# Other planning constants and thresholds in a four-layer attention kernel whose instruction order a planner lays out

## The chip, the cores and the metric

The kernel runs on one core of a Trainium2 chip. The core has five engines that run side by side and meet only at semaphores: TensorE (PE; matrix products, with PEld its weight loads), VectorE (DVE), ScalarE (ACT), GpSimd (POOL) and SyncE (SP). The metric is the device time of one execution in microseconds. Before the change it is 1484.73 us, the median of three runs (1484.37 to 1490.2).

## The reference

Four layers run over one sequence of 2048 rows of 512 columns, each with a layer norm in front and added to its input: softmax attention with 32 query heads of width 16 that share one key head and one value head (A), linear attention (B), and the same two once more.

```python
def _A_ref(x, wq, wk, wv, wo):
    q = heads(x @ wq)                  # 32 heads of 16
    k, v = x @ wk, x @ wv              # one head of 16 each
    scores = einsum("bhqd,bkd->bhqk", q, k) * 16 ** -0.5
    p = softmax(scores)
    return merge(einsum("bhqk,bkd->bhqd", p, v)) @ wo

def _B_ref(x, wqkv, wo):               # phi(t) = t + 1 if t > 0 else exp(t), plus 1e-6
    q, k, v = split_heads(x @ wqkv)
    kv, z = einsum("bhsd,bhse->bhde", phi(k), v), phi(k).sum(rows)
    return merge(phi(q) @ kv / (phi(q) @ z + 1e-6)) @ wo

x = x + _A_ref(layernorm(x), A_wq, A_wk, A_wv, A_wo)
x = x + _B_ref(layernorm(x), B_wqkv, B_wo)
x = x + _A_ref(layernorm(x), A_wq, A_wk, A_wv, A_wo)
x = x + _B_ref(layernorm(x), B_wqkv, B_wo)
```

Layers 0 and 2 (A) hold most of the work: each has 32 x 2048 x 2048 exponentials.

## The kernel before

**Blocks and segments.** An A layer is cut into blocks of 128 keys by 512 (head, query) columns, 2048 blocks a layer, 4096 in all. A segment (`Seg`, L356) holds the blocks of one query tile of 128 rows and one half of the heads, 64 blocks as a rule; in layer 2 the first tiles are cut into smaller ones. For each block TensorE makes the scores with an array cut by rows (L990, "row" mode, 32x128 tiles, up to four products at a time), an engine takes the exponential, and TensorE multiplies by V with an array cut by columns (L1044, "col" mode, 128x32 tiles, four products at a time) into one accumulator bank. Other products use the whole array ("full").

**Two ways to an exponential.** ScalarE takes groups of two or three blocks from a set of three PSUM banks in one instruction (L1170, output in PT buffers). VectorE takes single blocks: it adds a constant to the scaled score and writes the result as a 16-bit integer whose bits are a power of two in bf16 (L1256, output in FB buffers). That is coarse, so four shifted copies with weights 0.35, 0.30, 0.25 and 0.21 are summed: four VectorE blocks make a chunk of 128x2048, and three copies of the chunk are made with 32, 64 and 96 added to the integers. TensorE multiplies all four copies by weighted V tiles (VW). A VectorE block thus costs four value products and a ScalarE block one.

**Who makes the copies.** VectorE makes them with one instruction each (L1304). One of the three may be made by a transfer instead: GpSimd first issues a transfer that fills a buffer with the constant (`prime`, L1316, issued at L1328), and once the chunk is whole, a transfer that adds the chunk to it on the way (`dma_shift`, L1335, issued at L1337). This document calls the second one an addition. Each is 512 KB.

**The planner.** No engine decides anything on the chip. While the program is built, `Planner` (L36) plays the run through with a set duration for each operation, keeps a queue by priority for each engine, and writes down for each engine the order in which its operations started. That order is what the chip runs, with semaphores between the engines. So the constants in question never reach the chip; they change which engine takes a block, and the order. Constants the change touches:

- `SWITCH` (L384, used at L179): what TensorE is charged when the array's shape changes. A QK group is charged 0.22, a value group 0.222.
- `DXF` (L450) and `DTAIL` (L451), used at L1329 and L1338: how long an addition holds the transfer queue, and what passes after that until it has landed. Issue is charged 0.95 and a latency of 0.3, a prime holds the queue for 1.7. The reload of a weight (L676) uses `DTAIL` too.
- `TUNE` (L454), thresholds for layer 0 and layer 2. They are module globals; what layer 0 sets and layer 2 doesn't stays in force in layer 2 (L1098, L1100).

The thresholds, by what they decide:

- Whether VectorE takes a block. In place of the third block of a ScalarE group (`dve_split`, L1246): only if VectorE's urgent backlog is at most `BLS` and its whole backlog at most `BLT`. With a bank of its own beside a group (`dve_open`, L1240): backlog at most `BLO`. Alone (`alone`, L1266, called at L144): backlog at most `DXB`. A new chunk is opened only with more than `FBO` free buffers (L1229).
- From where it takes the block (`dve_pick`, L1207): from the end of a segment that is more than `CHT` blocks ahead of ScalarE (`ENDL` in the last segment), or, if the four column groups are uneven, more than `CHE`.
- When the copies are made (L1295): a copy waits while at most `FBS` buffers are free and segments ahead of it still have value products to issue (for small segments, more than `AHEAD` of them).
- Whether a copy becomes an addition (L1291): a buffer must be primed, the chunk must not lie in the last `DMIN` segments, and the planned transfer queue must be less than `DQ` us long. A buffer is primed (L1323) only if fewer than `NPRE` are, more than `FBP` are free, and ScalarE isn't in the last `DMIN` segments.
- `BACK` (L1116): how many segments before the end two borrowed weight buffers are called back. `STICK` (L166): by how much priority TensorE may be pulled from, to stay in the present one of "col" and "full". `LAG` (L70) keeps its value.

```python
if len(blk) == CHB and primed and si < len(segs) - DMIN and pl.dmaq < pl.now + DQ:
    ws.remove(DSH)
    dma_shift(blk, f_, hold, *primed.pop(0))
```

There are 18 buffers of a chunk's size at most (12 of them FB, the others borrowed from OBB, sacc, xn, wq and wo2 while those rest; traces name them so).

When TensorE would idle, the planner puts in products whose result nobody uses (`fill`, L1070, issued at L1089), so that the array doesn't fall silent.

Of the kernel before, what the change touches and what calls it, by code (L numbers as in the profile page):

```python
# [35 lines left out]
class Planner:  # L36
# [43 lines left out]
    def op(self, opts, reads=(), writes=(), prio=5.0, lat=0.08, dma=False, name="", join=None, mode="full", port=False, after=(), behind=(), xfer=None, trn=False):  # L80

        o = Op()
        o.opts, o.prio, o.users, o.done, o.end = opts, prio, [], False, None
        o.eng, o.fn, o.n, o.value, o.sem, o.signal, o.isdma = None, None, None, None, None, False, dma
        o.name = (name, lat)
        o.freed = False
        o.begun = None
        o.cols = 0
        o.mode = mode
        o.port = port  # L90
        o.xfer = xfer
        o.trn = trn
        deps = set()
        for k in reads:
            deps.update(self.ws(k))
        for k in list(writes) + list(after) + list(behind):
            deps.update(self.ws(k))
            deps.update(self.readers.get(k, ()))
        if join is not None:
            deps.update(join.deps)  # L100
            deps.discard(join)
        for k in writes:
            if join is not None and join in self.ws(k):
                self.writer[k] = self.ws(k) + [o]
            else:
                self.writer[k] = [o]
                self.readers[k] = []
        for k in list(reads) + list(after):
            if k not in writes:
                self.readers.setdefault(k, []).append(o)  # L110
        o.deps = deps
        o.left = 0
        chain = len(opts) == 1 and PE in opts
        for d in deps:
            if not (d.done or (chain and d.freed and d.eng == PE)):
                o.left += 1
                d.users.append(o)
        if o.left == 0:
            self._eligible(o)
        return o  # L120
# [26 lines left out]
    def _dispatch1(self, e):  # L147
# [4 lines left out]
        while h:  # L152
# [24 lines left out]
            if e == PE:  # L177
                if self.mode != o.mode:
                    dur += max(SWITCH - (self.now - self.until[e]), ROWIN if o.mode == "row" else 0.0)  # L179
                self.mode = o.mode  # L180
# [175 lines left out]
class Seg:  # L356
# [11 lines left out]
    def take(self, js, back=False):  # L368
# [12 lines left out]
QK_DUR = 0.22  # L381
PV_DUR = 0.222
QK_LAT = 0.438
SWITCH = 0.107  # L384
ROWIN = 0.025
PV_LAT = 0.215
EX_LAT = 0.185
# [3 lines left out]
LAG = 0.15  # L391
# [17 lines left out]
BLS = 1.4  # L409
BLO = 5.0  # L410
DXB = 2.0
BLT = 2.5
# [12 lines left out]
ENDL = 12  # L425
# [7 lines left out]
FBO = 2  # L433
FBS = 4
AHEAD = 20
CHT = 19
PSH = False
STICK = 0.8
PBL = 1.2
BACK = 2  # L440
PRING = 8
DSH = 1
DMIN = 4
NPRE = 2
EVEN = True
CHE = 8
AVOID = True
PGEN = 0.95
DPF = 1.7
DXF = 3.2  # L450
DTAIL = 2.0  # L451
DQ = 4.0
FBP = 4
TUNE = {0: {"CHE": 2, "AHEAD": 10, "BLS": 1.7, "FBP": 2, "NPRE": 1, "DMIN": 3, "LAG": 0.1, "STICK": 2.0, "FBO": 1, "FBS": 4, "BLO": 7.0, "DXB": 0.8, "BLT": 3.2},  # L454
        2: {"CHE": 6, "CHT": 16, "FBS": 2, "AHEAD": 15, "BLO": 3.5, "DXB": 2.5, "FBP": 3, "DMIN": 2, "STICK": 0.8, "LAG": 0.1, "DQ": 5.0}}


def bass_interleave_layers__grouped_kv_mqa__linear_attn_block__prompt_kernel(
# [111 lines left out]
    def guest(L, kind, i, h=None):  # L570
        return once((L, kind, i, h), home[kind, i]) if (kind, i) in home else ()
# [103 lines left out]
    def reload(dst, src, writes, prio, behind):  # L675
        return op({PO: (1.1, lambda e: e.dma_start(dst, src))}, writes=writes, prio=prio, lat=0.3, dma=True, behind=behind, xfer=(2.4, DTAIL))  # L676

# [34 lines left out]
    def fb_keys(i):  # L712
        return [("FB", i, h) for h in range(CHB)]
# [267 lines left out]
    def run_a(L):  # L981
# [23 lines left out]
        def spend(h, o):  # L1005
            h[0] -= 1
            if o not in h[1]:
                h[1].append(o)
            if h[0] == 0:
                pl.give_after(h[2], h[3], h[1])  # L1010
# [85 lines left out]
        def act_stream():  # L1096
            if L == 0:
                globals().update(TUNE[0])  # L1098
            yield ("flag", ("K", L, 0))
            globals().update(TUNE[L])  # L1100
            if L:
# [214 lines left out]
        def prime():  # L1316
# [6 lines left out]
            while state["si"] < len(segs) - DMIN:  # L1323
                if len(primed) >= NPRE or len(fb_pool.free) <= FBP or fb_pool.wait:
# [3 lines left out]
                o = op({PO: (PGEN, lambda e, g_=g_: e.dma_start(fbs[g_].bitcast(I16), cst.to_broadcast([P, CHB * 512])))}, reads=["cst"], writes=fb_keys(g_), prio=9.0,  # L1328
                       lat=0.3, dma=True, behind=guest(L, "FB", g_), xfer=(DPF, DTAIL))  # L1329
                primed.append((g_, o))  # L1330
# [4 lines left out]
        def dma_shift(blk, f_, hold, g_, o):  # L1335
            pl.stat["dma"] += 1
            o = op({PO: (PGEN, lambda e: e.dma_start(fbs[g_].bitcast(I16), fbs[f_].bitcast(I16), accum_op=ALU.add))}, reads=fb_keys(f_), writes=fb_keys(g_), prio=0.0, lat=0.3,  # L1337
                   dma=True, xfer=(DXF, DTAIL))  # L1338
            spend(hold, o)
# [601 lines left out]
```

## Time and profile before

| | before |
|---|---|
| median of 3 runs (lowest, highest) | 1484.73 us (1484.37, 1490.2) |
| profiled execution: its time / its span | 1484.35 us / 1482.5 us |
| busy: PE, DVE, ACT, POOL | 95%, 95%, 97%, 29% of the span |
| mean granted TensorE clock | 1.000 |
| exponentials on ScalarE (L1170) | 1364 instructions of two or three blocks, 1374.3 us |
| blocks on VectorE (L1256) | 1131 |
| copies by VectorE (L1304) | 639 |
| additions (L1337) / primes (L1328) | 216 / 218 |

How to read it: a line such as "L1337 POOL DMA_DIRECT2D" is the group of instructions that line 1337 of the kernel made on GpSimd. "x110" counts instructions, then follow busy time in us and the mean of one in ns, then the idle time of the engine right before them and what ended it. Instructions overlap: on ScalarE and VectorE the next one starts before the last one has written its end, so the time from start to start is shorter than the time of one. The view of windows gives each engine's busy time between two moments; asked for one line, it gives that line's. The chain of waits lists the work that ended last, piece by piece: start, us that the piece set the pace, engine, tile, line, count.

### The profile page before, as it was taken

Reading aid. Unit: us, or ns where it says so; the run is one execution under the profiler, and the core shown is the slowest. Engines: PE = TensorE matmul, PEld = TensorE weight load, DVE = VectorE, ACT = ScalarE, POOL = GpSimd, SP = SyncE. Lnnn points to the kernel's source line nnn. Section 1 sums busy time; section 2 is a strip of 40 time slices with the busy share of each in tenths; the row PEclk is TensorE's granted clock in tenths of the full one; section 3 lists DMA queues with packets and bytes.
Section 4 is the critical chain, followed back from the end, with each engine's and each line's share of the span. In section 5 each row is a group of like instructions: output and inputs, shape, how many; then the busy total and the mean of one; then the engine's idle time right before and its main releaser. Section 6 shows DMA issues by size and latency. Waiting matters only on the chain.

```text
span 1482.5 us, 40513 instructions
## 1 busy us (share of the span) xinstructions
PE 1415.0 (95%) x16387; PEld 512.6 (35%) x16387; DVE 1412.3 (95%) x2628; ACT 1441.2 (97%) x1536; POOL 424.9 (29%) x627
## 2 busy tenths in 40 slices
PE   7999999999999999999999999999999999999998
PEld 4433333333332323233644323333333333333235
DVE  7999999999999999998866899999999999999996
ACT  8999999999999999999799999999999999999996
POOL 5323333333333332300111223333323333223201
PEclk9999999999999999999999999999999999999999
DMA  4887898897888987710000458898879899879701
GB/s 116 229 205 194 185 212 188 203 215 179 195 204 197 217 192 168 187 43 2 2 2 2 104 136 200 201 211 205 212 188 226 201 211 215 203 183 216 172 1 58
DMA packets 76745, 240.14 MB, mean 162 GB/s; under 512 B 14993, under 2 KB 20113, under 8 KB 76562
## 3 DMA queue, kind: packets, MB, share of 16 engines
q0 software_dynamic: 62928, 229.14, 65.9%
q1 hardware_dynamic: 13634, 8.43, 2.0%
q8 instruction: 131, 2.15, 0.6%
q14 instruction: 52, 0.43, 0.1%
HBM read 120.62 MB, written 2.10 MB: 83 GB/s over the span
## 4 chain that ended last, share of the span: by engine, by line
PE 38%; DVE 35%; ACT 19%; issue 7%; POOL 1%; DMA 0%; ACTq 0%; DVEq 0%; POOLq 0%
PE ps L1044 15%; DVE FB L1256 14%; ACT PT L1170 12%; PE ps L990 12%; DVE FB L1304 7%; ACT xnT L1170 3%; PE ps L761 3%; PE ps L923 2%; PE ps L1089 2%; ACT OBB L1170 2%; PE ps L1410 2%; DVE wq L1256 1%; DVE xn L1256 1%; DVE sacc L1390 1%; PE ps L757 1%
## 5 line engine op out<-in xcount | busy, mean ns | idle before, releaser
L1170 ACT ACTIVATE PT<-ps 128x1024 bf16<-128x1024 f32 (+1 forms) x957 | 1004.8, 1163 | 5.4 <-PE ps L990 4.5
L1256 DVE TENSOR_SCALAR FB<-ps 128x512 int16<-128x512 f32 x852 | 558.0, 677 | 2.4 <-PE ps L990 1.6
L990 PE MATMUL ps<-QT,KM 32*128 32x512 bf16 x4096 | 534.6, 384 | 26.7 <-ACT PT L1170 14.9
L1044 PE MATMUL ps<-FB,VW 128*32 128x512 bf16 x3279 | 471.5, 385 | 10.9 <-ACT PT L1170 4.2
L1044 PE MATMUL ps<-PT,V 128*32 128x512 bf16 x2081 | 375.2, 386 | 4.0 <-DVE FB L1304 1.3
L990 PEld LDWEIGHTS ps<-QT,KM 32*128 32x128 bf16 x4096 | 134.2, 90 | 445.7 <-ACT PT L1170 216.0
L1170 ACT ACTIVATE xnT<-ps 128x1024 bf16<-128x1024 f32 (+1 forms) x240 | 261.0, 1162 | 1.0 <-PE ps L990 0.5
L1304 DVE TENSOR_SCALAR FB<-FB 128x2048 int16<-128x2048 int16 (+1 forms) x346 | 230.7, 674 | 0.0
L1337 POOL DMA_DIRECT2D FB<-FB x110 | 105.0, 955 | 334.3 <-DVE FB L1256 176.5
L1170 ACT ACTIVATE OBB<-ps 128x1024 bf16<-128x1024 f32 (+1 forms) x167 | 186.3, 1151 | 0.7 <-PE ps L990 0.6
L1044 PEld LDWEIGHTS ps<-FB,VW 128*32 128x32 bf16 x3279 | 115.8, 94 | 147.7 <-issue 81.3
L1328 POOL DMA_DIRECT2D FB<-shift_row x150 | 124.6, 831 | 45.2 <-PE ps L1044 23.9
L1089 PE MATMUL ps<-QT,V 128*32 128x512 bf16 (+6 forms) x548 | 132.7, 311 | 1.7 <-DVE sacc L1393 0.9
L1044 PEld LDWEIGHTS ps<-PT,V 128*32 128x32 bf16 x2081 | 91.3, 93 | 65.4 <-issue 36.7
L1044 PE MATMUL ps<-xnT,V 128*32 128x512 bf16 x522 | 105.1, 386 | 0.3 <-ACT PT L1170 0.3
L844 POOL TENSOR_SCALAR ve<-mv 128x1 f32<-128x1 f32 x64 | 29.5, 463 | 234.2 <-DVE mv L843 232.6
L1044 PE MATMUL ps<-OBB,V 128*32 128x512 bf16 x362 | 82.5, 387 | 1.8 <-ACT PT L1170 0.8
L761 PE MATMUL ps<-wqkv,xnT 128*32 128x512 bf16 x960 | 83.2, 383 | 0.8 <-DVE xnT L746 0.7
L1089 PEld LDWEIGHTS ps<-QT,V 128*32 128x32 bf16 x548 | 44.1, 95 | 56.8 <-issue 35.1
L1256 DVE TENSOR_SCALAR xn<-ps 128x512 int16<-128x512 f32 x80 | 52.7, 677 | 0.0
L1044 PE MATMUL ps<-xn,VW 128*32 128x512 bf16 x267 | 49.7, 385 | 1.8 <-ACT PT L1170 1.3
L1256 DVE TENSOR_SCALAR wq<-ps 128x512 int16<-128x512 f32 x75 | 49.3, 676 | 0.1
(221 smaller groups left out, 1805.8 us busy)
## 6 DMA issues: line engine op xcount, KB each, us to landing
FB<-shift_row POOLq DMA_DIRECT2D x150, 512.0 KB, 6.7
FB<-FB POOLq DMA_DIRECT2D x110, 512.0 KB, 6.0
sacc<-shift_row POOLq DMA_DIRECT2D x17, 512.0 KB, 6.9
wq<-shift_row POOLq DMA_DIRECT2D x16, 512.0 KB, 7.1
wo<-shift_row POOLq DMA_DIRECT2D x14, 512.0 KB, 7.1
xn<-shift_row POOLq DMA_DIRECT2D x14, 512.0 KB, 7.1
FB<-wq POOLq DMA_DIRECT2D x13, 512.0 KB, 6.1
wq<-FB POOLq DMA_DIRECT2D x12, 512.0 KB, 6.1
```

The lines of the kernel that those rows point to most:

```text
L761: ins = e.matmul(dst[c, :], lhsT=l[:, c], rhs=r, start=(k == 0), stop=(k == len(pairs) - 1))
L844: op({PO: (0.1, lambda e: e.tensor_scalar(out=ve[:, t:t + 1], in0=mv[:, t, 1:2], scalar1=1e-5, scalar2=None, op0=ALU.add))}, reads=[("mv", ...
L923: ins = e.matmul(dst[:, g * P:(g + 1) * P], lhsT=lhs(g, k), rhs=rhs(k), start=(k == 0), stop=(k == FT - 1))
L990: return e.matmul(bank(b), lhsT=KM[r, sg.par, kt * P:(kt + 1) * P], rhs=QT[r, sg.t, :], start=True, stop=True)
L1044: ins = e.matmul(ps[32 * j:32 * j + 32, ACC * 512:(ACC + 1) * 512], lhsT=V[:, kt, :] if w is None else VW[:, kt, w, :], rhs=ap, start=(k = ...
L1089: o = op({PE: (n / 2400.0, lambda e: e.matmul(ps[32 * j:32 * j + 32, b * 512:b * 512 + n], lhsT=V0[:], rhs=QT[:, sg.t, 0:n], start=st, sto ...
L1170: ex = op({AC: (0.051 + 0.4267 * n, lambda e, n=n, s_=s_, p_=p_: e.activation(pts[p_][:, 0:n * 512], ps[:, s_ * 512:(s_ + n) * 512], ACTF. ...
L1256: o = op({DV: (0.602, lambda e: e.tensor_scalar(out=dst.bitcast(I16), in0=bank(b), scalar1=VB, scalar2=VLO, op0=ALU.add, op1=ALU.max))}, w ...
L1304: o = op({en: (du, lambda e, w=w, g_=g_: e.tensor_scalar(out=fbs[g_][:, 0:n].bitcast(I16), in0=fbs[f_][:, 0:n].bitcast(I16), scalar1=float ...
L1328: o = op({PO: (PGEN, lambda e, g_=g_: e.dma_start(fbs[g_].bitcast(I16), cst.to_broadcast([P, CHB * 512])))}, reads=["cst"], writes=fb_keys ...
L1337: o = op({PO: (PGEN, lambda e: e.dma_start(fbs[g_].bitcast(I16), fbs[f_].bitcast(I16), accum_op=ALU.add))}, reads=fb_keys(f_), writes=fb_k ...
L1410: o = op({PE: (0.12, lambda e, c=c: e.transpose(ps[:, b * 512 + c * P:b * 512 + (c + 1) * P], src[:, c * P:(c + 1) * P], identF[:]))}, rea ...
```

## The change

Constants alone change. In the planner `SWITCH` goes from 0.107 to 0.112, `DXF` from 3.2 to 3.0 and `DTAIL` from 2.0 to 1.8; `TUNE` gets other thresholds. The description of the change gives 194 additions for the new order.

```diff
-SWITCH = 0.107
+SWITCH = 0.112
...
-DXF = 3.2
-DTAIL = 2.0
+DXF = 3.0
+DTAIL = 1.8
...
-TUNE = {0: {"CHE": 2, "AHEAD": 10, "BLS": 1.7, "FBP": 2, "NPRE": 1, "DMIN": 3, "LAG": 0.1, "STICK": 2.0, "FBO": 1, "FBS": 4, "BLO": 7.0, "DXB": 0.8, "BLT": 3.2},
-        2: {"CHE": 6, "CHT": 16, "FBS": 2, "AHEAD": 15, "BLO": 3.5, "DXB": 2.5, "FBP": 3, "DMIN": 2, "STICK": 0.8, "LAG": 0.1, "DQ": 5.0}}
+TUNE = {0: {"CHE": 4, "FBO": 1, "FBS": 2, "AHEAD": 10, "BLS": 1.0, "DXB": 1.6, "BLT": 3.2, "NPRE": 1, "STICK": 1.5, "BACK": 3, "ENDL": 6, "FBP": 5, "DMIN": 3, "DQ": 4.0, "LAG": 0.1},
+        2: {"CHE": 4, "FBO": 0, "BLO": 3.5, "FBP": 6, "DMIN": 4, "ENDL": 12, "FBS": 7, "DXB": 1.2, "DQ": 3.0}}
```

With what stays in force from layer to layer and from the defaults, the values that differ are:

| | layer 0 before | layer 0 after | layer 2 before | layer 2 after |
|---|---|---|---|---|
| CHE / CHT / ENDL | 2 / 19 / 12 | 4 / 19 / 6 | 6 / 16 / 12 | 4 / 19 / 12 |
| BLS / BLO / DXB | 1.7 / 7.0 / 0.8 | 1.0 / 5.0 / 1.6 | 1.7 / 3.5 / 2.5 | 1.0 / 3.5 / 1.2 |
| FBO / FBS / FBP | 1 / 4 / 2 | 1 / 2 / 5 | 1 / 2 / 3 | 0 / 7 / 6 |
| DMIN / DQ | 3 / 4.0 | 3 / 4.0 | 2 / 5.0 | 4 / 3.0 |
| AHEAD / STICK / BACK | 10 / 2.0 / 2 | 10 / 1.5 / 3 | 15 / 0.8 / 2 | 10 / 1.5 / 3 |

## Prediction

> **What bounds the kernel now.** I read the page's busy times first, then the windows of the two long stages in which VectorE takes blocks, then the same windows for single lines, and last the chain of waits and the list of waits.
>
> ```profile
> PE 1415.0 (95%) x16387; PEld 512.6 (35%) x16387; DVE 1412.3 (95%) x2628; ACT 1441.2 (97%) x1536; POOL 424.9 (29%) x627
> ...
> PE 38%; DVE 35%; ACT 19%; issue 7%; POOL 1%; DMA 0%; ACTq 0%; DVEq 0%; POOLq 0%
> ```
> ```profile
> 100.00:650.00 550.00, 528.30 (x6098) 171.19 (x6095) 547.76 (x982) 548.27 (x570) 170.90 (x225) 1.00 0.81 190
> 850.00:1400.00 550.00, 531.42 (x6197) 177.38 (x6197) 548.32 (x998) 546.81 (x578) 179.07 (x236) 1.00 0.85 200
> ```
>
> The second fence is the view of windows: a stretch of 550 us in layer 0 and one in layer 2, with the busy time of PE, PEld, DVE, ACT and POOL, the granted clock, the share of the DMA engines and GB/s. DVE and ACT are busy for 99.4 to 99.7% of both, the clock is 1.00, and transfers stay off the chain (DMA 0%). TensorE only looks nearly as full: its dummy products (L1089) run where it has nothing else to do, 61.38 and 49.58 us in the two stretches:
>
> ```profile
> 100.00:650.00 550.00, 61.38 (x262) 21.09 (x262) 1.00 0.81 190
> 850.00:1400.00 550.00, 49.58 (x207) 16.64 (x207) 1.00 0.85 200
> ```
>
> So two engines share 2048 blocks a layer and neither has a hole. The length of these stages is the work of ScalarE and VectorE over what both can do, and an order can shorten them only by making that work smaller. The four next rows are of the stage of layer 0 and that of layer 2, for the additions (L1337) and VectorE's copies (L1304), then the totals for VectorE's blocks (L1256) and ScalarE's exponentials (L1170):
>
> ```profile
> 41.00:701.60 660.60, 104.29 (x109) 1.00 0.76 178
> 832.00:1445.00 613.00, 102.39 (x107) 1.00 0.79 185
> 41.00:701.60 660.60, 224.44 (x335) 1.00 0.76 178
> 832.00:1445.00 613.00, 199.20 (x304) 1.00 0.79 185
> 41.00:701.60 660.60, 387.13 (x592) 1.00 0.76 178
> 832.00:1445.00 613.00, 350.07 (x537) 1.00 0.79 185
> sum 1482.50, ACT 1374.28; mean ACT 274.86
> ```
>
> They close: in layer 0, 592 blocks are 148 chunks of four, with three copies each 444, and 335 + 109 = 444. VectorE takes 592 + 537 and two more between the stages, 1131, and ScalarE the other 4096 - 1131 = 2965.
>
> **The change part by part.** *Prices.* The chain of waits shows VectorE's operations start to start:
>
> ```profile
> 652.40 0.60 DVE sacc L1501
> 653.00 1.39 DVE FB L1304 x2
> 654.39 1.19 DVE FB L1256 x2
> 655.58 0.60 DVE FB L1304
> 656.18 1.20 DVE FB L1256 x2
> ```
>
> A block and a copy of a chunk cost 0.60 us each. A block on VectorE with all three copies made there costs (4 + 3) x 0.60 / 4 = 1.05 us; a block on ScalarE costs 1374.28 / 2965 = 0.46 us.
>
> *Fewer additions.* Of 109 + 107 = 216 additions 194 would be left, 22 fewer. `DMIN` in layer 2 accounts for some: two more segments of 613 / 32 = 19 us without additions, at 107 in 613 us, are 7. The rest would come from `FBP` (fewer primes) and `DQ` (3.0 for 5.0). Each one dropped is a copy for VectorE, 22 x 0.60 = 13.2 us. Nothing hides that, since VectorE has 2 us of idle in 550. It is shared, though: if VectorE gives y blocks to ScalarE, both end later by 0.46 y = 13.2 - 1.05 y, so y = 8.7 and the end moves by 4.0 us, a share of 0.31 of any work added to VectorE (0.69 for ScalarE). Bounds: 1.3 us if only `DMIN`'s 7 count (7 x 0.60 x 0.31), 4.0 for all 22; I take 4.0, since the count is given. GpSimd loses 44 issues, and TensorE 8.7 x 3 / 4 value groups, about 1.4 us; both have room.
>
> *Shorter planned transfers.* An addition is planned to land 0.95 + 0.3 + 3.2 + 2.0 = 6.45 us after it starts, behind an empty queue, and after the change 6.05. The view of line L1337 and the list of waits say:
>
> ```profile
> who waited for it (us, times):
>   PEld ps L1044: 0.2, 1
> ...
> DMA to landing us min/median/max: 4.6/6.0/9.1
> ```
> ```profile
> PEld ps L1044 <- DVE FB L1304: 17.3, 64, 0.8
> ```
>
> Today TensorE waits once, 0.2 us, for an addition. Planned 0.4 us earlier, value products move up by as much, and about half the landings (those above the median, 6.0) come after the plan. In TensorE's order the score products for the next group stand behind such a wait, and ScalarE waits for those. Lower bound nothing; upper bound 97 waits of 0.4 us, 39 us. TensorE waits 17.3 us for VectorE's copies today, the same kind of wait, while ScalarE is idle 4.9 us in the 1100 of the two stretches whatever the cause, so at most 39 x 4.9 / 17.3 = 11 us would reach ScalarE, 8 us of time. I take 1 us, near the row of 0.2. The Trainium skill, DMA: Bandwidth & Descriptors, section "Anatomy of one DMA — SWDGE (gpsimd) path", fits 2.0 us plus bytes / 436e3 us to such a transfer, which for 512 KB is an estimate of 3.2 us; by it both plans are pessimistic and this term is nothing, a sum 1 us lower. The trace disagrees, at a median of 6.0.
>
> *Shape changes.* In the chain near 50 us TensorE's pieces are
>
> ```profile
> 50.54 0.32 PE ps L990 x3
> 50.87 0.33 PE ps L1044 x4
> 53.85 0.76 PE ps L1044 x12
> 55.59 0.55 PE ps L1044 x8
> ```
>
> One, two and three groups of four cost 0.33, 0.55 and 0.76, so a group is 0.215 and the change of shape 0.11. The plan's score group with its switch goes from 0.220 + 0.107 = 0.327 to 0.332, against 0.32: 5 ns on each change, on an engine with 111 us of dummy products in the two stretches. Nothing.
>
> *Backlog thresholds* (`BLS`, `BLO`, `DXB`). Splits set how many of ScalarE's groups have two blocks instead of three. In the timeline of ScalarE
>
> ```profile
> 319.21 1.02 ACT L1170 ACTIVATE OBB<-ps 128x1024 bf16<-128x1024 f32 x1
> 320.14 1.45 ACT L1170 ACTIVATE PT<-ps 128x1536 bf16<-128x1536 f32 x1
> 321.49 1.02 ACT L1170 ACTIVATE OBB<-ps 128x1024 bf16<-128x1024 f32 x1
> ...
> 682.70 1.96 ACT L1170 ACTIVATE PT<-ps 128x1024 bf16<-128x1024 f32 x2
> 684.51 1.07 ACT L1170 ACTIVATE OBB<-ps 128x1024 bf16<-128x1024 f32 x1
> ```
>
> a group of three takes 1.35 us (0.45 a block) and one of two 0.905 to 0.93 (0.45 to 0.465). If a tenth of the 2965 blocks changed the size of its group, that is 297 x 0.015 = 4.5 us of ScalarE, 3 us of time either way; I take nothing.
>
> *Ends of the stages* (`ENDL`, `CHE`, `CHT`, `BACK`). At the end of layer 0 VectorE's last copies and ScalarE's last group are
>
> ```profile
> 698.30 1.28 DVE L1304 TENSOR_SCALAR FB<-FB 128x2048 int16<-128x2048 int16 x2
> 700.38 1.15 ACT L1170 ACTIVATE PT<-ps 128x1024 bf16<-128x1024 f32 x1
> ```
>
> They stop 1.95 us apart (699.58 and 701.53). There is at most that to win, and about a chunk's copies (3 x 0.60) to lose: 2 us either way, taken as nothing. What runs from 701.6 to 832 and after 1445 is untouched but for its order.
>
> **The sum.** The profiled execution took 1484.35 us (1482.5 of span, the rest around it), 0.38 under the median of the runs: 1484.35 + 4.0 + 1.0 = 1489.4. I forecast 1489 us. Its own range, with the ends of the four open terms (1.3 to 4.0; 0 to 8; 3 either way; 2 either way, taken as unlikely to fall together), is 1483 to 1494.
>
> **The rivals.**
> *A, the buffers starve VectorE.* In layer 2 `FBS` 2 to 7 holds back the copies of any chunk whose segment isn't due while seven or fewer of the 18 buffers are free, and `FBP` 6 the primes. Copies have the lowest priority and are what fills VectorE today (304 in layer 2 beside 537 blocks). If they wait and no bank is free for a new block, VectorE idles, and later they come in a heap in front of the value products. At 5% of the stage's 613 us that is 31 us, 9 us of time: 1499. It decides from about 8 us of idle, where the loss goes over 7.4 us with the forecast's terms; now it is 1.7 us in 550. Against it: the planner would take new blocks instead, and `FBO` 0 lets it open chunks to the last buffer.
> *B, the lost additions cost nothing.* VectorE is busy 92.84 us of the 130.4 between the stages, and 41.89 of the last 45 of layer 2, where `DMIN` drops its share; if the dropped ones fall where it idles, or a better end of the layers pays for them, the time stays at 1485.
>
> ```profile
> 701.60:832.00 130.40, 126.38 (x1559) 67.14 (x1555) 92.84 (x216) 116.32 (x129) 20.99 (x52) 1.00 0.03 9
> 1400.00:1445.00 45.00, 41.82 (x500) 14.60 (x495) 41.89 (x78) 44.58 (x45) 2.54 (x3) 1.00 0.06 16
> ```
>
> Against it: copies can't be moved into the 130 us, where VectorE has no blocks of the layer left.
> *C, faster: ScalarE's groups start on time.* Idle of under the time by which instructions overlap doesn't show as idle. At 0.905 for two, 2965 blocks would take 1342 us, and their lines take 1374.28; the 32 us are late starts, score products held up behind a change of shape. If truer prices and `STICK` 1.5 in layer 2 win half of that, 16 x 0.69 = 11 us, the time is 1484.35 + 4.0 - 11 = 1477. It needs 6 us of the 32 to break even with the lost additions. Against it: the plan's price of a switched group was right within 7 ns already, and a late start is a matter of two sets of banks, which stay. That the order stays as it was, so that nothing changes, is excluded by the count of 194.
>
> **How the numbers follow.** Chances: the forecast 0.45, A 0.22, B 0.18, C 0.15. A change of under 0.5%, 7.4 us, can't be told from none here: faster ends at 1477.3, slower begins at 1492.1. Of the forecast, 0.13 lies above 1492.1 and 0.32 within; of A, 0.20 above; B lies within; of C, 0.13 below. Slower 0.33, same 0.02 + 0.32 + 0.18 + 0.02 = 0.54, faster 0.13. The range from 1478 to 1499 leaves out half of C and half of A, together 0.18.
>
> **What would show it.** L1337 should count 194 and L1304 grow by some 15, less three quarters of the lost L1256 blocks, which fall by about 9; ScalarE's and VectorE's busy shares in the two stretches stay above 99%. The second term shows as waits of PEld L1044 for additions, of 1 to 10 us in total where there is 0.2. A shows as idle of VectorE above 8 us in layer 2; C as less than 0.46 us of L1170 a block. I am wrong if time falls while the additions do, or if the stretches open holes of several per cent.

## The result, and the profile after

The kernel after the change takes 1490.84 us (median of 14 runs, 1487.34 to 1493.86), the kernel before 1485.38 us (median of 14, 1484.37 to 1492.44). The ratio is 1.003, 95% interval 1.002 to 1.004: slower, by less than the 0.5% that the prediction set as its bound. The forecast was 1489 us, its range 1478 to 1499. The profiled execution of the kernel after took 1491.47 us, with a span of 1489.7.

The page of the kernel after, its busy times and the engines' shares of the chain of waits:

```profile
PE 1423.1 (96%) x16364; PEld 513.3 (34%) x16368; DVE 1412.5 (95%) x2619; ACT 1448.7 (97%) x1538; POOL 393.0 (26%) x583
...
DVE 34%; PE 32%; ACT 19%; issue 8%; DMA 4%; POOL 1%; SPq 0%; ACTq 0%; POOLq 0%; DVEq 0%
```

The busy shares look as before. The chain doesn't: transfers, 0% of it before, are 4%. The view of windows for the same two stretches (PE, PEld, DVE, ACT, POOL, granted clock, share of the DMA engines, GB/s), then the additions (L1337) in the stages of layer 0 and layer 2, VectorE's copies (L1304) and VectorE's blocks (L1256) in the same two, and ScalarE's exponentials (L1170):

```profile
100.00:650.00 550.00, 527.02 (x6061) 172.12 (x6057) 544.88 (x977) 547.58 (x566) 170.87 (x219) 1.00 0.80 186
850.00:1400.00 550.00, 529.45 (x6116) 173.81 (x6116) 544.27 (x987) 547.37 (x572) 152.49 (x203) 1.00 0.73 169
...
41.00:705.00 664.00, 102.30 (x105) 1.00 0.73 172
832.00:1452.50 620.50, 83.78 (x89) 1.00 0.66 154
...
41.00:705.00 664.00, 226.91 (x339) 1.00 0.73 172
832.00:1452.50 620.50, 206.46 (x310) 1.00 0.66 154
...
41.00:705.00 664.00, 387.72 (x587) 1.00 0.73 172
832.00:1452.50 620.50, 349.29 (x528) 1.00 0.66 154
...
sum 1490.00, ACT 1381.57; mean ACT 1381.57
```

105 + 89 = 194 additions, 4 fewer in layer 0 and 18 fewer in layer 2. VectorE makes 649 copies for 639 and takes 1115 blocks for 1131, so ScalarE takes 2981, at 1381.57 / 2981 = 0.463 us each, as before (1374.28 / 2965 = 0.4635). Two engines are still close to full: VectorE idles 5.1 and 5.7 us in the stretches (2.2 and 1.7 before), ScalarE 2.4 and 2.6 (1.7 and 3.2 before).

The view of line L1337 of the kernel after, and the rows of its list of waits that matter (engine, tile and line that waits, what it waits for: us in total, times, the longest):

```profile
who waited for it (us, times):
  PEld ps L1044: 8.9, 22
  PE ps L1044: 2.9, 5
  POOL FB L1328: 1.8, 1
...
DMA to landing us min/median/max: 4.5/5.8/9.7
```
```profile
PEld ps L1044 <- DVE FB L1304: 13.3, 53, 0.8
...
PEld ps L1044 <- DMA FB<-FB: 4.4, 12, 1.2
```

Weight loads for value products wait 22 times for an addition, 8.9 us, where before it was once and 0.2 us; the waits for VectorE's copies are shorter (13.3 us for 17.3). The transfers have not become slower: the median from start to landing is 5.8 us for 6.0. Their results are called for sooner, as the experiments with the plan alone bear out below. What one such wait does is seen in the chain of waits and the timeline of the kernel after around the longest one (start, us, engine, line, and in brackets the idle time before with what ended it):

```profile
113.92 7.19 DMA FB<-FB
```
```profile
119.98 1.02 ACT L1170 ACTIVATE OBB<-ps 128x1024 bf16<-128x1024 f32 x1
120.17 0.68 DVE L1256 TENSOR_SCALAR FB<-ps 128x512 int16<-128x512 f32 x1
121.15 0.10 PEld L1044 LDWEIGHTS ps<-FB,VW 128*32 128x32 bf16 x4 [1.18 <-DMA FB<-FB]
121.15 0.40 PE L1044 MATMUL ps<-FB,VW 128*32 128x512 bf16 x4 [0.89 <-DMA FB<-FB]
121.48 0.10 PEld L990 LDWEIGHTS ps<-QT,KM 32*128 32x128 bf16 x3 [0.23 <-issue]
121.48 0.39 PE L990 MATMUL ps<-QT,KM 32*128 32x512 bf16 x3
...
121.92 1.02 ACT L1170 ACTIVATE OBB<-ps 128x1024 bf16<-128x1024 f32 x1 [0.91 <-PE ps L990]
121.92 0.69 DVE L1256 TENSOR_SCALAR FB<-ps 128x512 int16<-128x512 f32 x1 [1.07 <-PE ps L990]
```

This addition took 7.19 us, where the plan had 6.05. The value products (L1044) stand in TensorE's queue ahead of the score products (L990), which don't need the addition. They wait with them, and both of the full engines stand still for about a microsecond until the scores are there. An accounting by waits shows this as an idle of ScalarE ended by PE; the transfer is one step further back.

### The profile page after: what moved, and what is told of

Read it like the earlier page. It is cut to its first block, busy times and chain, and to the rows that moved or that the text cites. A ratio compares the mean times of both kernels' runs of the same rounds, so it can differ in the third digit from the quotient of the medians.

```text
span 1489.7 us, 40296 instructions
## 1 busy us (share of the span) xinstructions
PE 1423.1 (96%) x16364; PEld 513.3 (34%) x16368; DVE 1412.5 (95%) x2619; ACT 1448.7 (97%) x1538; POOL 393.0 (26%) x583
## 4 chain that ended last, share of the span: by engine, by line
DVE 34%; PE 32%; ACT 19%; issue 8%; DMA 4%; POOL 1%; SPq 0%; ACTq 0%; POOLq 0%; DVEq 0%
ACT PT L1170 14%; DVE FB L1256 12%; PE ps L1044 12%; PE ps L990 10%; DVE FB L1304 7%; ACT xnT L1170 2%; PE ps L1089 2%; PE ps L923 2%; DVE xn L1256 2%; PE ps L761 2%; ACT OBB L1170 2%; PE ps L1410 2%; DMA FB<-FB 1%; DVE OBB L1256 1%; DVE sacc L1390 1%
## 5 line engine op out<-in xcount | busy, mean ns | idle before, releaser
L1170 ACT ACTIVATE PT<-ps 128x1024 bf16<-128x1024 f32 (+1 forms) x959 | 1007.2, 1175 | 4.7 <-PE ps L990 3.6
L990 PE MATMUL ps<-QT,KM 32*128 32x512 bf16 x4096 | 534.8, 385 | 24.3 <-ACT PT L1170 12.1
L1256 DVE TENSOR_SCALAR FB<-ps 128x512 int16<-128x512 f32 x776 | 515.0, 685 | 5.1 <-PE ps L990 4.3
L1044 PE MATMUL ps<-FB,VW 128*32 128x512 bf16 x3241 | 462.9, 385 | 13.6 <-ACT PT L1170 3.6
L1044 PE MATMUL ps<-PT,V 128*32 128x512 bf16 x2110 | 371.3, 388 | 5.7 <-ACT PT L1170 3.8
L990 PEld LDWEIGHTS ps<-QT,KM 32*128 32x128 bf16 x4096 | 134.6, 91 | 444.2 <-ACT PT L1170 209.8
L1170 ACT ACTIVATE xnT<-ps 128x1024 bf16<-128x1024 f32 (+1 forms) x237 | 249.8, 1147 | 1.4 <-PE ps L990 1.2
L1304 DVE TENSOR_SCALAR FB<-FB 128x2048 int16<-128x2048 int16 (+1 forms) x324 | 217.8, 681 | 0.3
L1170 ACT ACTIVATE OBB<-ps 128x1024 bf16<-128x1024 f32 (+1 forms) x167 | 187.0, 1150 | 1.6 <-PE ps L990 1.5
L1337 POOL DMA_DIRECT2D FB<-FB x95 | 92.4, 973 | 337.1 <-DVE FB L1256 204.2
L1044 PEld LDWEIGHTS ps<-FB,VW 128*32 128x32 bf16 x3241 | 114.1, 94 | 146.4 <-issue 74.4
L1089 PE MATMUL ps<-QT,V 128*32 128x512 bf16 (+6 forms) x577 | 139.2, 313 | 0.4 <-DVE xn L1256 0.2
L1044 PEld LDWEIGHTS ps<-PT,V 128*32 128x32 bf16 x2110 | 90.9, 94 | 80.0 <-issue 40.8
L1044 PE MATMUL ps<-xnT,V 128*32 128x512 bf16 x506 | 105.5, 386 | 1.2 <-ACT xnT L1170 0.8
L1044 PE MATMUL ps<-OBB,V 128*32 128x512 bf16 x365 | 83.4, 389 | 2.4 <-ACT PT L1170 2.0
L1256 DVE TENSOR_SCALAR xn<-ps 128x512 int16<-128x512 f32 x96 | 63.5, 682 | 0.3 <-PE ps L990 0.2
L1044 PE MATMUL ps<-xn,VW 128*32 128x512 bf16 x261 | 55.5, 385 | 1.0 <-DVE sacc L1390 0.9
L1256 DVE TENSOR_SCALAR wq<-ps 128x512 int16<-128x512 f32 x80 | 53.7, 686 | 1.0 <-PE ps L990 0.6
```

The source lines that it names most:

```text
L990: return e.matmul(bank(b), lhsT=KM[r, sg.par, kt * P:(kt + 1) * P], rhs=QT[r, sg.t, :], start=True, stop=True)
L1044: ins = e.matmul(ps[32 * j:32 * j + 32, ACC * 512:(ACC + 1) * 512], lhsT=V[:, kt, :] if w is None else VW[:, kt, w, :], rhs=ap, start=(k = ...
L1089: o = op({PE: (n / 2400.0, lambda e: e.matmul(ps[32 * j:32 * j + 32, b * 512:b * 512 + n], lhsT=V0[:], rhs=QT[:, sg.t, 0:n], start=st, sto ...
L1170: ex = op({AC: (0.051 + 0.4267 * n, lambda e, n=n, s_=s_, p_=p_: e.activation(pts[p_][:, 0:n * 512], ps[:, s_ * 512:(s_ + n) * 512], ACTF. ...
L1256: o = op({DV: (0.602, lambda e: e.tensor_scalar(out=dst.bitcast(I16), in0=bank(b), scalar1=VB, scalar2=VLO, op0=ALU.add, op1=ALU.max))}, w ...
L1304: o = op({en: (du, lambda e, w=w, g_=g_: e.tensor_scalar(out=fbs[g_][:, 0:n].bitcast(I16), in0=fbs[f_][:, 0:n].bitcast(I16), scalar1=float ...
```

## The experiments

Ratios are against runs of the kernel before on the same chip; on the three chips its medians are 1485.16 to 1485.46 us, so that times can be set side by side. The first expectation names three theories of what the 5.46 us are: the copies that fall back to VectorE (1), the start (2), and late landings (3). One thing bears on all the times: the granted clock differs a little between executions of the same program. Of 67 runs of the kernel before, the 28 with a mean clock of 1.000 have a median of 1484.68 us; at 0.998 it took 1486.5 to 1487.7, at 0.994 1490.4 to 1490.6, so about 1 us for each 0.001.

| kernel | additions | waits of PEld L1044 for them, us (times) | median, us | ratio, 95% interval |
|---|---|---|---|---|
| before | 216 | 0.2 (1) | 1485.38 | |
| after | 194 | 8.9 (22) | 1490.84 | 1.003 (1.002 to 1.004) |
| b_sw112 | 216 | 3.3 (8) | 1484.28 | 0.9994 (0.9985 to 1.0002) |
| a_sw107 | 196 | 12.4 (21) | 1495.89 | 1.0066 (1.0050 to 1.0082) |
| a_short | 194, short | none | 1485.70 | 0.9999 (0.9991 to 1.0008) |
| b_short | 216, short | none | 1484.99 | 0.9997 (0.9988 to 1.0006) |
| b_noadd | 0 | | 1529.02 | 1.0287 (1.0267 to 1.0307) |
| b_dxdt | 227 | 5.0 (9) | 1490.89 | 1.0034 (1.0021 to 1.0046) |
| b_dxdt_short | 227, short | none | 1488.70 | 1.0016 (1.0004 to 1.0027) |
| a_dxdt | 185 | 0.5 (1) | 1493.42 | 1.0051 (1.0039 to 1.0064) |
| a_sw107_short | 196, short | 0.2 (1) | 1488.30 | 1.0024 (1.0015 to 1.0033) |
| b_dtail05 | 219 | 40.2 (61) | 1520.90 | 1.0228 (1.0191 to 1.0264) |
| best_a | 237 | 0.3 (1) | 1479.15 | 0.9950 (0.9933 to 0.9967) |
| best_b | 225 | 4.9 (9) | 1480.37 | 0.9965 (0.9950 to 0.9979) |

The waits are those of one profiled execution each. "Short" additions move 512 of the 2048 columns in the very order of the kernel they are named after, so that three quarters of the constants are left out of the result; everything else is the same.

**The charge for a change of shape, put into the kernel before (b_sw112).**

```diff
-SWITCH = 0.107
+SWITCH = 0.112
```

> The kernel before with SWITCH 0.112 alone: 216 additions and nearly the same number of VectorE blocks (1133 for 1131), but the order of the first 40 us is that of the changed kernel up to the first VectorE blocks. Theory 1 (the loss is the copies that fall back to VectorE, 0.18 us for each addition lost): no addition is lost, so 1484 to 1487 us. Theory 2 (part of the loss is the start: the new order leaves TensorE emptier there and the granted clock falls to 0.5 for one or two stretches of 3.4 us): clock below 1.000 in most runs, first VectorE block near 45 us instead of 41.6, and 2 to 4 us longer, 1487 to 1490 us. Theory 3 (TensorE waits for additions that land after their planned time): TensorE waits under 1 us for additions, as before, and 1485 us.

1484.28 us, no difference. The profiled execution ran at a clock of 1.000 and took its first VectorE block at 42.9 us, as late as the orders that carry the thresholds of after. Here a start 1.3 us later did not make the kernel slow, and the charge alone costs nothing. Theory 3 missed in one point: it expected waits under 1 us, and there are 3.3. At the price of a wait found below they would be 1 to 2 us, which this order makes up elsewhere.

**The charge taken back out of the kernel after (a_sw107).**

```diff
-SWITCH = 0.112
+SWITCH = 0.107
```

> The changed kernel with SWITCH back at 0.107: 196 additions for 194, thresholds and planned transfers as changed, but the order of the first 40 us is that of before. Theory 1: 20 additions fewer than before, 1485.4 + 3.6 = 1489 us. Theory 2: clock 1.000 in all runs, first VectorE block at 41.6 to 42 us, and 2 to 4 us less than the changed kernel, 1487 to 1489 us. Theory 3: TensorE still waits 8 to 15 us in total for additions, and the time stays at 1490 to 1492 us.

A miss for both theories: 1495.89 us, 5 us over the kernel after, with the first VectorE block back at 41.6 us and a clock of 1.000. This ends the theory of the start. In the order that came out TensorE waits longer still for additions, though they land no later (5.9 us at the median); the view of line L1337 of this kernel says

```profile
  PEld ps L1044: 12.4, 21
  PE ps L1044: 6.7, 11
```

**Late landings taken out of the kernel after, its order kept (a_short).** A transfer of a quarter of the columns lands far ahead of its plan, and nothing else in the order moves.

```diff
-e.dma_start(fbs[g_].bitcast(I16), fbs[f_].bitcast(I16), accum_op=ALU.add)
+e.dma_start(fbs[g_][:, 0:512].bitcast(I16), fbs[f_][:, 0:512].bitcast(I16), accum_op=ALU.add)
```

> The order of the changed kernel, instruction for instruction, but each addition moves one block of the chunk (512 of 2048 columns) instead of four, so that it lands sooner; three quarters of the added constants are left out of the result. Theory 3: the waits of TensorE for additions fall from 11.8 us to under 1 us and the time by 3 to 6 us, to 1485 to 1488 us. Theories 1 and 2: the waits fall in the same way, but the time stays within 1.5 us of the changed kernel, 1489 to 1492 us, since VectorE has the same copies to make and the start is the same.

1485.70 us, 5.14 below the kernel after. The view of line L1337, which names no one who waited, and the two stretches:

```profile
who waited for it (us, times):
...
DMA to landing us min/median/max: 2.6/2.8/5.7
```
```profile
100.00:650.00 550.00, 528.48 (x6077) 172.60 (x6075) 546.40 (x982) 548.76 (x569) 168.24 (x218) 1.00 0.45 116
850.00:1400.00 550.00, 531.45 (x6138) 174.44 (x6130) 544.99 (x989) 548.53 (x575) 151.21 (x201) 1.00 0.40 106
```

With nothing landing late the kernel after is back at the time of the kernel before (ratio 0.9999). ScalarE gets 1.2 us of each stretch back (547.58 to 548.76 and 547.37 to 548.53). VectorE, though, idles 5.0 us in layer 2 even so, where it was 1.7 before: most of that hole is not of late landings.

**The same edit in the kernel before (b_short)**, as a control for what less traffic is worth by itself.

> The order of the kernel before, instruction for instruction, with each addition moving one block (512 of 2048 columns) instead of four; three quarters of the added constants are left out of the result. It is the control for the same edit to the changed order, which took 5.1 us off. Theory 3 (the changed order loses by waits for additions that land late): this order waits 0.2 us for additions, so the time stays within 1 us of 1485.3 us. Rival (shorter additions help any order, through the transfer queue or memory): 3 to 6 us less here too, 1480 to 1482 us.

1484.99 us, against 1485.38: with no late landings to remove, short additions save 0.4 us at most. So the 5.14 us of a_short are not traffic. The medians split the 5.46 that were measured into 1490.84 - 1485.70 = 5.14 for the landings, 1485.70 - 1484.99 = 0.71 for all the rest of the change, and 1484.99 - 1485.38 = -0.39 for the shortening; such a chain of differences adds up whatever the cause, and what carries it is the control.

Some of the 5.14 is clock: 10 of the 14 runs of the kernel after had a mean clock under 1.000, 4 of the 11 of a_short; of the kernel before it was 39 of 67. The four runs of after at 1.000 took 1487.34, 1488.41, 1488.69 and 1493.86 (median 1488.55), the seven of a_short 1484.82 to 1485.86 (median 1485.42), the four of b_short 1484.61 to 1484.91 (median 1484.6), and those of the kernel before have a median of 1484.68. At equal clock, then, the change costs 3.9 us, and 3.1 of them are the landings. The two profiled executions agree: their spans, 1489.7 and 1483.8, are 5.9 us apart, of which 2.4 are there at VectorE's first block (45.3 and 42.9 us), ahead of any addition, at a clock of 0.50 for two stretches (last section). The other 3.5 come later. The landings cost 3 to 4 us at equal clock; whether waits for them ever bring the lower clock about, these runs don't tell.

**No additions at all (b_noadd).** The thresholds of before, with the additions and primes shut off.

```diff
-"DMIN": 3 (layer 0), "DMIN": 2 (layer 2)
+"DMIN": 99 in both
```

> The kernel before with DMIN 99 in both layers, so that no chunk qualifies: 0 additions for 216, all copies on VectorE, the planner sharing out the blocks anew. Theory 1: 216 x 0.60 x 0.31 = 40 us longer, 1520 to 1530 us, with 90 to 100 VectorE blocks fewer. Rival (the additions take work off an engine that has room elsewhere, so that they are worth little): under 1500 us.

1529.02 us: (1529.02 - 1485.3) / 216 = 0.20 us for each addition lost. Its four runs had clocks of 0.993 to 0.999; the one at 0.999, 1525.17 us, gives 0.18. VectorE makes 798 copies for 639 and takes 1039 blocks for 1131, 0.43 fewer for each addition. It is nearly as full as before in layer 0 (546.00 of 550) and less so in layer 2 (541.02), so a part of the price is idle time:

```profile
100.00:650.00 550.00, 520.74 (x5874) 172.80 (x5876) 546.00 (x981) 547.12 (x542) 17.60 (x26) 1.00 0.01 2
850.00:1400.00 550.00, 527.05 (x5906) 178.06 (x5904) 541.02 (x985) 542.54 (x546) 16.11 (x27) 0.99 0.01 2
```

**The plan of a transfer, alone (b_dxdt, a_dxdt).** In the kernel before the shorter plan goes in; in the kernel after it comes out.

```diff
 b_dxdt                      a_dxdt
-DXF = 3.2                  -DXF = 3.0
-DTAIL = 2.0                -DTAIL = 1.8
+DXF = 3.0                  +DXF = 3.2
+DTAIL = 1.8                +DTAIL = 2.0
```

> The kernel before with DXF 3.0 and DTAIL 1.8 alone: 227 additions for 216, thresholds and SWITCH as before. Theory 1 (the count of additions sets the time, 0.20 us each): 2 us less, 1483 us. Theory 3: TensorE waits 8 to 20 us for additions, as in the two kernels with these values, and the time is 2 to 7 us longer than by count alone, 1486 to 1491 us.

1490.89 us. Eleven additions more than before should have saved 11 x 0.20 = 2.2; it is some 5 us slower, with 5.0 us of waits for landings, fewer than the 8 to 20 expected.

> The changed kernel with DXF 3.2 and DTAIL 2.0 back, so that only SWITCH and the thresholds are changed: 185 additions. Theory 1: 31 additions fewer than before at 0.20 us, 1485.3 + 6.2 = 1491.5 us. Theory 3: the waits for additions fall under 4 us, which takes back 3 to 5 us, while 9 additions fewer than in the changed kernel cost 1.8: 1487 to 1489.5 us.

A miss for theory 3: 1493.42 us. The longer plan does away with the waits, as a_short did, but the planner answers with 185 additions, 31 fewer than before. Counted from the kernel before that is 31 x 0.20 = 6.2 and 1491.6, the number of theory 1, and the other 2 us are within what the clock of its five runs explains, 0.997 to 0.999. Counted from a_short, which has the same thresholds and no waits, nine additions fewer would give only 1487.5. So this order is some 4 us worse at like clock than that of a_short, for reasons that neither count nor landings hold. The two views of line L1337, b_dxdt first:

```profile
  PEld ps L1044: 5.0, 9
  PE ps L1044: 2.4, 4
```
```profile
  PEld ps L1044: 0.5, 1
  PE ps L1044: 0.3, 1
```

**Two more orders with short additions (a_sw107_short, b_dxdt_short)**, each its namesake with the edit of a_short, to see how far lateness explains the slow ones.

> The order of the changed kernel with SWITCH 0.107, which took 1495.9 us and waited 19 us for additions, with each addition moving one block instead of four; three quarters of the added constants are left out of the result. Theory 3: the waits go, and most of the 10 us over the kernel before with them: 1486 to 1489 us. Rival (that order is bad in itself, by the shape changes that SWITCH misprices): 1493 to 1496 us.

1488.30 us, 7.6 below a_sw107: its extra cost over the kernel after was mostly landings. It stays 2.6 over a_short with two additions more, which is the order itself.

> The order of the kernel before with DXF 3.0 and DTAIL 1.8 (227 additions, 1490.9 us, 7.4 us of waits for additions), with each addition moving one block instead of four; three quarters of the added constants are left out of the result. Theory 3: the 5.7 us over the kernel before are mostly late landings, and go with them: 1484 to 1487 us. Rival (this order is worse in itself, whatever the landings): 1489 to 1491 us.

1488.70 us, 2.2 below b_dxdt, and partly a miss: 3.7 over b_short with eleven additions more. Here half of the loss or more is the order that the planner found under its new prices, and no late landing.

**A plan that is far too short (b_dtail05).**

```diff
-DTAIL = 2.0
+DTAIL = 0.5
```

> The kernel before with DTAIL 0.5 for 2.0 alone: 219 additions, planned to land 1.5 us sooner than before, which is 1 us sooner than the median landing. A larger dose of the same. Theory 3: waits of TensorE for additions of 30 to 70 us in total, at 0.4 to 0.7 us of time for each, 1500 to 1530 us. Theory 1: 3 additions more, 1485 us.

1520.90 us, 35 us slower with 219 additions. The view of line L1337 of this kernel, and its stretch in layer 0:

```profile
  PEld ps L1044: 40.2, 61
  PE ps L1044: 20.1, 35
```
```profile
100.00:650.00 550.00, 518.24 (x5977) 168.18 (x5976) 540.70 (x964) 540.87 (x558) 177.63 (x230) 1.00 0.84 195
```

Now the holes open where the prediction's upper bound looked for them: VectorE and ScalarE each idle over 9 us in 550, and the traffic (195 GB/s) is no more than before (190). Some 8 of the 35 us are clock: the four runs had 0.990 to 0.999, and the one at 0.999 took 1512.97. At like clock, the loss per us of wait was 3.1 / 8.9 = 0.4 in after, (1494.79 - 1488.28) / 12.4 = 0.5 in a_sw107 (a single run at 1.000), (1490.2 - 1487.4) / 5.0 = 0.6 in b_dxdt, and (1512.97 - 1485.37) / 40.2 = 0.7 here, this one with whatever its order cost besides.

Set side by side, the plans show the dose: with additions planned to land in 6.45 us the waits are 0.2 to 4.9 us (before, b_sw112, a_dxdt, best_a, best_b), in 6.05 us 5.0 to 12.4 (b_dxdt, after, a_sw107), in 4.95 us 40.2.

**Two other orders under the prices of before (best_a, best_b).** `SWITCH`, `DXF` and `DTAIL` stay as in the kernel before; only thresholds differ, chosen for more additions. Shown are the values in force that differ, without the quotes of the code.

```diff
 best_a
-        0: CHE 2, AHEAD 10, BLS 1.7, FBP 2, DMIN 3, FBS 4, BLO 7.0, DXB 0.8, DQ 4.0
+        0: CHE 6, AHEAD 8, BLS 1.2, FBP 1, DMIN 0, FBS 1, BLO 4, DXB 1.6, DQ 5.0
-        2: CHT 16, FBS 2, AHEAD 15, BLO 3.5, DXB 2.5, DMIN 2, NPRE 1, FBO 1, BACK 2, BLS 1.7
+        2: CHT 14, FBS 1, AHEAD 12, BLO 3.0, DXB 1.6, DMIN 0, NPRE 2, FBO 0, BACK 1, BLS 1.0
 best_b
-        0: CHE 2, CHT 19, AHEAD 10, BLS 1.7, NPRE 1, DMIN 3, FBO 1, BLO 7.0, BACK 2
+        0: CHE 5, CHT 20, AHEAD 15, BLS 1.0, NPRE 2, DMIN 2, FBO 0, BLO 5, BACK 1
-        2: AHEAD 15, DMIN 2, FBO 1, ENDL 12, BLS 1.7
+        2: AHEAD 10, DMIN 1, FBO 0, ENDL 10, BLS 1.0
```

> The kernel before, with its own planned transfers and SWITCH, and thresholds that let 237 chunks have an addition, 21 more than before (DMIN 0 in both layers, FBP 1 in layer 0, NPRE 2 in layer 2). Theory 1: 21 x 0.20 us less, 1481 us. Theory 3: landing times planned as before, so waits for additions under 5 us, which would take back 2 us at most. Rival (transfers this dense land later than planned): waits over 10 us and 1485 us or more.

1479.15 us, 1477.87 to 1480.40 apart from one run of 2256.28 whose cause isn't known: it beats both kernels, by 6 us the one before. With 21 additions more than before, 21 x 0.20 = 4.2 of it is the count. Its view of line L1337 and its two stretches, in which VectorE idles 1.2 and 5.9 us:

```profile
  PEld ps L1044: 0.3, 1
...
DMA to landing us min/median/max: 4.5/6.1/9.1
```
```profile
100.00:650.00 550.00, 525.60 (x6106) 170.03 (x6107) 548.77 (x983) 549.25 (x568) 184.93 (x242) 1.00 0.89 207
850.00:1400.00 550.00, 528.80 (x6138) 175.30 (x6136) 544.10 (x989) 545.63 (x576) 177.01 (x233) 1.00 0.84 197
```

> A second set of thresholds on the constants of before, with 225 additions, 9 more, and nine VectorE blocks fewer. By the count 1483.4 us; how far it and the kernel with 237 lie from their counts shows how much two orders with like counts differ on the chip: by up to 3 us, if the kernel of 196 additions without late landings (1488.3 us) and that of 194 (1485.7 us) are a measure.

1480.37 us with 225 additions, where the count gives 1485.4 - 9 x 0.20 = 1483.6, and that in spite of 4.9 us of waits. Its one run at a clock of 1.000 took 1477.57, 7.1 under the kernel before at that clock, of which the count explains 1.8. Orders with like counts differ by 3 to 5 us for reasons that neither count nor landings hold.

## Why the prediction was right, and where it wasn't

Time and sign came out as forecast, but the sum was lucky: two terms were mis-sized in opposite directions. Late landings, put at 1.0, cost 3.1 us at equal clock and 5.1 by the medians; thresholds and ends, put at 0, stand where some 3 to 4 us were won back.

**Fewer additions, +4.0.** The price holds: 0.18 to 0.20 us an addition by b_noadd, where the prediction had 4.0 / 22 = 0.18, and 0.43 blocks go to ScalarE for each, where it had 8.7 / 22 = 0.40. In the profiled executions of before and a_short, both at a clock of 1.000, layer 2 from its first to its last exponential takes 717.58 and 721.36 us: +3.8 with 18 additions fewer, where 18 x 0.20 = 3.6. Yet all of the change without its late landings comes to 0.71 us, not 4.4. The rest was given back: against 4 x 0.20 = 0.8 us to be lost, layer 0 takes 2.5 us less from VectorE's first block to its last exponential (659.97 and 657.44), and the stretch from there to layer 2's first exponential 1.3 less (25.73 and 24.39), while the start takes 1.3 more.

**Thresholds and ends, 0.** In the prediction's sum only these terms, taken as nothing with bounds of 3 and 2 either way, are left to hold those 3 to 4 us. That the thresholds by themselves won them is not shown: a_dxdt has the same thresholds and lies where the count puts it, and a_sw107_short, at 1488.28 for a clock of 1.000, has won back 1 us at most. The gain belongs to the one order that all the constants together gave, and it is of the size by which orders differ anyhow. Why that order gains in layer 0 stays open.

**Shorter planned transfers, +1.0.** The mechanism was as told, late landings in an in-order queue with score products behind; the waits, 8.9 us, lie inside the 1 to 10 that were to show it. The step that failed is the price of a wait: the prediction let 4.9 / 17.3 of it reach ScalarE, from the waits for copies, and chose a value near the single wait of 0.2. Measured at like clock, a us of wait costs 0.4 to 0.7, and the term is 3.1 us (5.1 by the medians), inside its upper bound of 8. Waits for copies were a poor model: 64 of them in 17.3 us are 0.27 each, the 22 for landings 0.40 each with one of 1.18. Nor did half of the landings hold TensorE up, as the upper bound of 97 waits had it: there were 22 waits for 194 additions. The Trainium skill, DMA: Bandwidth & Descriptors, section "Anatomy of one DMA — SWDGE (gpsimd) path", would have made this term nothing, as its fit, an estimate of 3.2 us for 512 KB, undercuts both plans; the runs say 5.8 to 6.1 at the median and up to 10.6 (best_b).

**Shape changes, 0.** Right for the charge by itself (b_sw112). In the company of other constants the same 5 ns gave an order 5 us away (a_sw107): the cost of such a constant is that it makes the planner find another order.

**A, starved buffers.** VectorE's idle in layer 2 did grow, to 5.7 us for 1.7, under the 8 from which A decides. Without late landings it is still 5.0, and a_dxdt, with the same thresholds and hardly a wait, has 4.2. That the thresholds starve it a little, (5.0 - 1.7) x 0.31 = 1.0 us by the prediction's share, is worked out and not tried alone; best_a idles 5.9 us there with other thresholds and is the fastest of all.

**B, lost additions cost nothing.** As a mechanism refuted by b_noadd and supported by nothing; its number, 1485, is nevertheless where the order stands once the landings are on time (1485.70), since layer 0 and the stretch behind it paid for layer 2. **C, a punctual ScalarE.** Not seen: 0.463 us a block, as before.

**The rest of what was to show it.** L1337 counts 194 as said. L1304 grew by 10, where 15 less three quarters of 9 blocks made 8; L1256 fell by 16 for 9. The 99% of busy time held for ScalarE, with 99.5%; VectorE has 99.07 and 98.96%, so that it fell just short in layer 2. GpSimd lost 44 instructions (627 and 583), as many as said.

## What to carry to other kernels

Where a plan is executed in order, the planned time of a transfer shouldn't be close to its median. Here TensorE then waited 22 times for 194 additions, each wait stopped what stood behind it in the queue, and that cost 0.4 to 0.7 us for each us of wait, while a plan that is too long costs the work that the free helper could have taken, about 0.20 us an addition. To price lateness, keep the order and make the transfer short: planning again with other constants moves the time by 3 us or more for reasons of its own, which hid the answer in a_sw107, b_dxdt and a_dxdt. And a sum that comes out right deserves the same experiments as one that doesn't, since two of its terms may be wrong against each other.

## What the runs showed of the hardware

A transfer that adds 512 KB from one buffer to another lands 6.0 us after its start (median of the kernel before), one of 128 KB in 2.8: 384 KB in 3.2 us, 0.12 MB a us. A straight line through these two medians, an estimate, leaves a fixed part of about 1.7 us.

The profiled execution of the kernel after lost time at its start to the clock. The view of windows (columns as above) around 22 to 39 us:

```profile
22.00:25.30 3.30, 2.80 (x39) 1.22 (x35) 3.04 (x10) 3.30 (x4) 1.78 (x5) 1.00 0.56 113
25.40:28.80 3.40, 3.40 (x25) 0.65 (x25) 3.09 (x9) 3.15 (x3) 2.48 (x7) 0.50 0.22 43
28.90:32.10 3.20, 2.81 (x39) 1.25 (x35) 2.77 (x9) 2.62 (x3) 0.90 (x2) 1.00 0.00 0
32.20:35.60 3.40, 3.40 (x31) 0.74 (x29) 1.65 (x6) 2.80 (x3) 2.17 (x6) 0.50 0.40 81
```

Two stretches of 3.4 us have a clock of 0.50, one window apart, and its first VectorE block comes at 45.3 us where the same order at full clock (a_short) has it at 42.9. Such stretches fall in some executions of one order and not in others. The profiled execution of the kernel before has a clock of 1.00 in all of its first 46 us and its first VectorE block at 41.6 us; that of b_short, which has the same order and a mean clock of 0.997, has three of them and its first block at 45.1:

```profile
25.80:29.20 3.40, 3.38 (x28) 0.83 (x25) 2.33 (x7) 3.12 (x4) 2.54 (x7) 0.50 0.21 43
29.20:32.60 3.40, 3.37 (x27) 1.43 (x28) 3.05 (x9) 2.68 (x3) 1.19 (x3) 0.50 0.19 39
32.60:36.00 3.40, 3.40 (x27) 1.36 (x26) 1.67 (x5) 2.63 (x3) 1.33 (x3) 0.52 0.38 77
```

All of this lies ahead of the first addition (issued at 47.5 us in before, 50.9 in b_short, 50.6 in after), so no wait for one brought it about. The Trainium skill, TensorE: Matmul & The Clock Gate, section "What's actually happening", has a free-running window of 3413 ns and a half rate for the idle state; the length and the rate agree with these rows. In the kernel after, TensorE was not idle ahead of the first stretch but busy for 2.80 of 3.30 us, and a_short, at full clock, was busy for the same 2.80 us there.
